# An FFT convolution's last tile: its intermediate results stored and reloaded in seven groups instead of three, and its inverse transform in three parts

## The chip, the cores and the metric

The kernel runs on one core of one Trainium2 chip. The metric is the device time of one execution in microseconds (us). Engines are named as in the profile: PE (TensorE), DVE (VectorE), ACT (ScalarE), POOL (GpSimd) and SP (SyncE, which here only issues DMAs). Every engine works through its own list in order.

## What is computed

A 7 x 7 convolution of a 224 x 224 image with 96 channels, as a product of Fourier transforms. The filter is padded with zeros and the product is circular, so it is a circular convolution:

```python
x: (1, 224, 224, 96) bf16, w: (7, 7, 96, 96) bf16
wp = jnp.pad(w, ((0, H - K), (0, W - K), (0, 0), (0, 0)))
Xf = rfft2(x.astype(float32), axes=(1, 2))
Wf = rfft2(wp.astype(float32), axes=(0, 1))
Yf = jnp.einsum('bhwi,hwio->bhwo', Xf, Wf)
y = irfft2(Yf, s=(H, W), axes=(1, 2)).astype(bfloat16)
```

## The kernel before

The image is cut into 8 bands of 28 rows (NJ, B). Along the rows a short transform of length 34 with 17 frequency slots (NS) is used; along the width the 7 taps are applied directly, with ten taps in a fast form for pairs of pixels. The width is cut into seven tiles of 32 pixels, t = 0 to 6; the last is TL = 6.

Each tile goes through three stages, which overlap between tiles.

- A: PE transforms the rows of x by matmuls with Fm; ACT and DVE evict the result from PSUM into xf. DVE then makes differences and sums of planes (J) by groups of slots (JGB).
- B, `b_round(t, s, ...)`, once for each slot s: PE multiplies the planes with the filter's slots (WF) into two PSUM banks. ACT scales the first bank into a tile `tt__` (in the two real slots, 0 and 16, it copies). DVE makes u and v from `tt__` and the banks. The sum of u and v goes to yf: on DVE in some slots, else on POOL. In the last tile DVE has slots 0, 3, 6, 9, 12 and 14 to 16, and POOL has 1, 2, 4, 5, 7, 8, 10, 11, 13. The rounds of one tile are the slots 0 to 16.
- C: the sums of a group of slots are stored from yf to scratch in DRAM (scr), since the inverse transform contracts over slots and bands and so needs another layout. They are reloaded with bands, slots and real or imaginary part on the partitions; PE multiplies with G; ACT and DVE evict; SP stores to out. For tiles 0 to 5 this work of tile t - 1 is spread over the rounds of tile t as jobs (`c_jobs`), with stores from the buffers yo and J.

The last tile's C stage has no later tile beside which it could run. Its groups of slots are in YGRPL. A group's store is made by `put` at the group's last slot; in the last tile, all but the last are put into the list `puts` and are issued by ACT one round later, right behind the scale of that round, by `puts.pop(0)()`. The last one is issued by SP. The scratch of the last tile is three tensors: slots 0 to 8 (scra, up to SA), 9 to 14 (scrb, up to SB), and 15 and 16 (a second scrb). SP reloads the first in round 11 (SA + 2), in four DMAs; after the rounds `load_b` reloads the second on ACT in two halves, and the third on SP.

The inverse of the last tile is 16 chunks of 384 columns with two matmuls each. `first` multiplies the reloaded slots 0 to 8 (72 partitions: four bands) with GA and needs only the first reload; `second` multiplies slots 9 to 16 (128 partitions: eight bands) with GB and adds to the same PSUM bank. Eight firsts are issued, then WARM = 36 matmuls of 384 columns with zeros that add nothing, then the seconds, each followed by its eviction by DVE or ACT in turn (`tail_evac`) and, after the fourth, by the first of a later chunk. Every second chunk SP stores 768 columns of 112 rows to out. GA and GB are made from G by 20 small DMAs, one for each round of tiles 3 and 4 (`g_parts`).

All engines' lists are in the program's own order (`_Ordered`). An instruction that waits holds all that stand behind it on its engine; a DMA also waits for the DMA eight before it, since eight semaphores are used in turn. PSUM has eight banks, given out in turn by `bank()`.

Of the kernel before, what the change touches and what calls it, by code (L numbers as in the profile page):

```python
# [8 lines left out]
BF16 = mybir.dt.bfloat16  # L9
# [5 lines left out]
B = 28  # L15
L = B + KT - 1
LC = L - 2
NS = L // 2
REAL = (0, NS - 1)
JG = 4  # L20
NJ = 8
# [3 lines left out]
TW = 16  # L25
# [7 lines left out]
NSLOT = 2 + 3 * (NS - 1)  # L33
PGRP = ((0, 5), (5, 8), (8, 11), (11, 14), (14, 17))
YGRP = ((0, 3), (3, 6), (6, 9), (9, 12), (12, 15), (15, 17))
YGRPL = ((0, 3), (3, 6), (6, 9), (9, 12), (12, 15), (15, 17))
SA = 9
SB = 15
YMAX = 3
YBUF = 4  # L40
JGB = ((0, 3), (3, 6), (6, 9), (9, 12), (12, 15), (15, 17))
# [2 lines left out]
SH2 = (0, 8, 13, 17)  # L44
MERGE = ()
NP2 = 0
WARM = 36
FILL = 3
FEV = 4
WMID = 14  # L50
# [16 lines left out]
def kernel(  # L67
# [50 lines left out]
    def bank():  # L118
        return pools["psb"].tile([128, 512], F32, name="pb")
# [36 lines left out]
    KA = 4 * 2 * SA  # L156
    KB = (NJ * 2 * (SB - SA), NJ * 2 * (NS - SB))
    assert sum(KB) == 128
    XW = 2 * TW * C
    xn_bufs = [cpool.tile([R, XW + 32], BF16, name=f"xn{i}") for i in range(2)]  # L160

# [52 lines left out]
    wu = cpool.tile([128, 128], BF16, name="wu")  # L214
# [341 lines left out]
    def b_round(t, s, mid, end, ydve=False, planes=()):  # L556
# [26 lines left out]
        if s in REAL:  # L583
            for part in range(2):
                conv(b0, part * C, 0, part)
            SE.copy(out=tt_[:, 0:2 * C], in_=b0[:, 0:2 * C])
            mid()
            for mi, m in enumerate((2, 1)):
                for part in range(2):
# [52 lines left out]
            load["v"] += (560 if ydve else 250 if t < 2 else 0) + (560 if merge else 900)  # L642
            end()
        if s == y1 - 1:
            dst, yo0 = scr_tiles[t], 0
            if t == TL:
                i = (s >= SA) + (s >= SB)
                dst, yo0 = scr_tiles[(t, i)], (0, SA, SB)[i]
# [25 lines left out]

    TW2 = 2 * TW * C
    tl_all = xf_bufs[(TL + 1) % 2].rearrange("c p r s w j -> c (p r s w j)")
    tl_a = [tl_all[0:KA, g * TW2:(g + 1) * TW2].rearrange("p (w e) -> p w e", e=2 * C) for g in range(2)]
    tl_b = tl_all[:, 2 * TW2:3 * TW2].rearrange("p (w e) -> p w e", e=2 * C)

    def load_b(i, eng, nh):  # L680
        sb = scr_tiles[(TL, 1 + i)].rearrange("w j s (r e) -> (j s r) w e", r=2)
        for h in range(nh):
            w0, w1 = h * TW // nh, (h + 1) * TW // nh
            eng.dma_start(out=tl_b[i * KB[0]:i * KB[0] + KB[i], w0:w1], in_=sb[:, w0:w1])

    def g_parts():
        for j in range(4):
            dma(GA[j * 2 * SA:(j + 1) * 2 * SA, j * B:(j + 1) * B], G[0:2 * SA, 0:B])
            yield
        for j in range(NJ):  # L690
# [128 lines left out]
    for r in range(NS + LAG):  # L819
        if r == 0:  # L820
            for i in range(2, PGRP[0][1]):
                add(2 * i - 4, 2 * i - 3, [diff(i)])
            add(1, 4, fj[1][1])
            add(3, 7, fj[2][1])
        for p in range(3):
            if r == (1, 3, 5)[p]:
                new_xf(1, SH2[p], SH2[p + 1])
                fj = f_jobs(1, p)
                if p == 2:
                    for jg in range(2):  # L830
                        fj[jg][-1] = then_load(fj[jg][-1], 2, jg)
                add(2 * r + 1, 2 * r + (5, 5, 4)[p], fj[0] + fj[1])
        for p in range(3):
            if r == SH2[p + 1] + 1 - (p == 2):
                new_xf(2, SH2[p], SH2[p + 1])
                fj = f_jobs(2, p)
                if p == 2:
                    for jg in range(2):
                        fj[jg][-1] = then_load(fj[jg][-1], 3, jg)
                add(2 * r, 2 * r + (8, 7, 5)[p], fj[0] + fj[1])  # L840
        if r == PGRP[-2][1] + 1:
            assert not any(q[2] for q in qs[:len(PGRP) - 1])
# [5 lines left out]
            GA = g_pool.tile([KA, 4 * B], BF16, name="GA")  # L848
            GB = g_pool.tile([128, 2, 4 * B], BF16, name="GB")
            GE.memset(GA[:], 0.0)  # L850
            GE.memset(GB[:], 0.0)
# [18 lines left out]
    gp = g_parts()  # L870
    for t in range(2, NT):
        if t == TL:
            scr_tiles[t] = None
            scr_tiles[(t, 0)] = dr_pool.tile([TW, NJ, SA, 4 * C], BF16, name="scra")
            for i in range(2):
                scr_tiles[(t, 1 + i)] = dr_pool.tile([TW, NJ, (SB - SA, NS - SB)[i], 4 * C], BF16, name=f"scrb{i}")
        else:
            scr_tiles[t] = dr_pool.tile([TW, NJ, NS, 4 * C], BF16, name="scr")
        qs = []
# [38 lines left out]

    def first(g, q):
        pc = bank()[0:M4, 0:4 * C]  # L920
        TE.matmul(pc, lhsT=GA[:], rhs=tl_a[g][:, 2 * q:2 * q + 2, :].rearrange("p w e -> p (w e)"), start=True, stop=False)
        return pc

    def second(g, q, pc, yo):
        TE.matmul(pc, lhsT=GB[:, g], rhs=tl_b[:, 2 * q:2 * q + 2, :].rearrange("p w e -> p (w e)"), start=False, stop=True)
        tail_evac(yo[0:M4, q % 4 * 4 * C:(q % 4 + 1) * 4 * C], pc, 4 * C)
    order = [(g, q) for h in range(2) for g in range(2) for q in range(4 * h, 4 * h + 4)]
    live = {k: first(*k) for k in order[:8]}
    for _ in range(WARM):
        TE.matmul(live[order[7]].rearrange("p (a b) -> p a b", a=3), lhsT=wu[:, 0:M4], rhs=wu[:].unsqueeze(1).to_broadcast([128, 3, 128]),  # L930
                  start=False, stop=False)
    LF = 4
    for i, (g, q) in enumerate(order):
        if q % 4 == 0:
# [5 lines left out]
        if q % 2 == 1:  # L940
            w0, c0 = TL * 2 * TW + (q - 1) * 4, (q % 4 - 1) * 4 * C
            dma(out[0, g * M4:(g + 1) * M4, w0:w0 + 8, :].rearrange("h w c -> h (w c)"), yo[0:M4, c0:c0 + 8 * C])
    if not NP2:
        ps0_cm.__exit__(None, None, None)

# [29 lines left out]
```

## Time and profile before

| | us |
|---|---|
| median of 3 runs (268.49 to 272.28) | 268.77 |
| the profiled execution, its own time | 269.31 |
| its span, first to last instruction | 267.5 |
| PE busy | 255.1 (95%) |
| DVE busy | 216.2 (81%) |
| ACT busy | 197.6 (74%) |
| POOL busy | 97.7 (37%) |
| round 0 of the last tile: ACT's copy starts | 222.61 |
| round 16 of the last tile: ACT's copy starts | 250.11 |
| first and last store of the last tile's output are issued | 259.56, 263.42 |

The mean granted clock of TensorE is 0.995. DMA moves 46.78 MB at a mean of 175 GB/s. The profile shows one execution. All work has the line of one helper (L101), so that rows are told apart by the names of the tiles: out<-in, partitions x elements, type. A busy time is the time from an instruction's start to its end; instructions of one engine overlap a little, so that starts follow each other faster than the durations tell. "SPq" and "ACTq" are DMA issues.

### The profile page before, as it was taken

To read this page: it belongs to the slowest core of one execution; us is meant where nothing else is said; L and a number is where in the kernel's file an instruction comes from. 1 tells how busy PE (TensorE), PEld (TensorE's weight loads), DVE (VectorE), ACT (ScalarE), POOL (GpSimd) and SP (SyncE) were. 2 spreads that over 40 slices of the span, in tenths; PEclk is the share of its full clock that TensorE was granted. 3 is DMA by queue.
4 is the path that set the end of the run, shared out by engine and by line. 5 is a ranking of instruction groups with operands and counts; after the bars stand their busy time and mean duration, and the time that the engine had idled before them with its cause. 6 is when DMAs were issued, how large, how long until landed. Compare 5 with 4: busy or idle time off the path is not lost. (4 is left out here: it accounts for less than half of the span.)

```text
span 267.5 us, 12139 instructions
## 1 busy us (share of the span) xinstructions
PE 255.1 (95%) x5128; PEld 235.7 (88%) x5128; DVE 216.2 (81%) x465; ACT 197.6 (74%) x485; POOL 97.7 (37%) x152
## 2 busy tenths in 40 slices
PE   8897999999999999999999999999999999999983
PEld 2787999999998999999999998989999889879861
DVE  7997699889899788778887888778888789978523
ACT  8796978497964578998988789886988864187123
POOL 7771324364558344222222322233123323422100
PEclk9999999999999999999999999999999999999998
DMA  8994102711111697987876486979678443887845
GB/s 197 230 251 76 48 2 67 245 45 48 47 48 49 192 258 159 294 238 223 272 195 188 117 235 221 253 216 341 235 152 242 169 128 125 204 250 182 259 107 191
DMA packets 46690, 46.78 MB, mean 175 GB/s; under 512 B 35292, under 2 KB 38056, under 8 KB 46540
## 3 DMA queue, kind: packets, MB, share of 16 engines
q1 hardware_dynamic: 44348, 43.95, 59.6%
q10 hardware_dynamic: 2288, 2.06, 2.6%
q8 instruction: 40, 0.66, 1.1%
q14 instruction: 14, 0.11, 0.2%
HBM read 24.66 MB, written 21.33 MB: 172 GB/s over the span
## 5 line engine op out<-in xcount | busy, mean ns | idle before, releaser
L101 PE MATMUL pb<-WF,J 96*128 96x96 bf16 x2821 | 162.9, 206 | 1.7 <-DVE J L101 1.3
L101 PEld LDWEIGHTS <-J 96*128 96x128 bf16 x2821 | 138.0, 98 | 12.3 <-issue 3.5
L101 POOL TENSOR_TENSOR yf<-v,u 128x384 bf16<-128x384 f32 x79 | 81.3, 1040 | 145.7 <-issue 84.6
L101 ACT CAST xf<-pb 96x408 bf16<-96x408 f32 (+3 forms) x145 | 67.3, 486 | 7.6 <-PE pb L101 3.8
L101 PE MATMUL pb<-WF,xf 96*128 96x96 bf16 x952 | 60.0, 206 | 0.9 <-ACT WF L101 0.9
L101 DVE TENSOR_TENSOR J<-xf 96x1824 bf16<-96x1824 bf16 (+1 forms) x84 | 56.9, 716 | 0.0
L101 PEld LDWEIGHTS <-xf 96*128 96x128 bf16 x952 | 47.2, 98 | 1.3 <-issue 1.2
L101 PE MATMUL pb<-Fm,xn 118*128 118x136 bf16 (+3 forms) x640 | 45.5, 199 | 0.2 <-DVE u L101 0.2
L101 PE MATMUL pb<-tt,Gm 102*84 102x384 bf16 (+1 forms) x132 | 32.9, 326 | 0.6 <-ACT J L101 0.3
L101 PEld LDWEIGHTS <-xn 118*128 118x128 bf16 x640 | 30.3, 97 | 0.3 <-issue 0.3
L101 ACT CAST WF<-pb 96x480 bf16<-96x480 f32 (+1 forms) x58 | 28.6, 558 | 2.3 <-PE pb L101 2.3
L101 ACT CAST J<-pb 84x384 bf16<-84x384 f32 (+1 forms) x65 | 28.1, 490 | 2.6 <-PE pb L101 2.6
L101 ACT CAST yo<-pb 84x384 bf16<-84x384 f32 (+1 forms) x63 | 27.1, 486 | 2.3 <-POOL yf L101 1.3
L101 DVE TENSOR_TENSOR J<-J 96x912 bf16<-96x912 bf16 (+2 forms) x42 | 24.2, 576 | 0.0
L101 PE MATMUL pb<-wq 128*128 128x120 bf16 (+1 forms) x288 | 21.8, 226 | 0.7 <-DMA wq<-in_w_dram 0.6
L101 PEld LDWEIGHTS <-wq 128*128 128x128 bf16 (+1 forms) x288 | 19.9, 148 | 1.7 <-DVE xf L101 1.1
L101 DVE TENSOR_TENSOR yf<-v,u 128x384 bf16<-128x384 f32 x26 | 15.1, 580 | 0.9
L101 PE MATMUL pb<-wu 128*112 128x384 bf16 (+1 forms) x59 | 14.5, 391 | 1.1 <-DVE ct L101 1.1
L101 PEld LDWEIGHTS <-wu 128*112 128x112 bf16 (+1 forms) x59 | 7.4, 127 | 5.6 <-issue 3.1
L101 PEld LDWEIGHTS <-Gm 102*84 102x84 bf16 (+1 forms) x132 | 11.1, 117 | 1.0 <-issue 0.4
L101 ACT COPY xf<-xf 96x816 bf16<-96x816 bf16 (+3 forms) x20 | 11.1, 613 | 0.0
L101 ACT CAST tt<-pb 112x384 bf16<-112x384 f32 x8 | 3.6, 480 | 9.3 <-PE pb L101 9.2
(387 smaller groups left out, 239.2 us busy)
## 6 DMA issues: line engine op xcount, KB each, us to landing
scr<-yf SPq DMA_DIRECT2D x30, 288.0 KB
xn<-in_x_dram SPq DMA_DIRECT2D x12, 672.0 KB
tt<-scr SPq DMA_DIRECT2D x24, 336.0 KB
out_dram<-yo SPq DMA_DIRECT2D x12, 252.0 KB
out_dram<-J SPq DMA_DIRECT2D x12, 252.0 KB
tt<-scr SPq DMA_DIRECT2D x6, 288.0 KB
WF<-in_x_dram SPq DMA_DIRECT2D x2, 672.0 KB
out_dram<-tt SPq DMA_DIRECT2D x8, 168.0 KB
```

Of the source, the lines that this page charges most:

```text
L101: r = fn(*a, **k)
```

## The change

The last tile's slots are stored in seven groups with a scratch tensor each: slots 0 to 2, 3 to 5, 6 and 7, 8 to 10, 11 to 13, 14 and 15, and 16 alone. The groups are reloaded onto the partitions of three parts: part 0 takes the first three groups (128 partitions), part 1 the next two (96), part 2 the last two (48). All eight bands are on the partitions in each. SP reloads the first five groups in the rounds 5, 8, 10, 13 and 16, each at the head of its round; after the rounds ACT reloads slots 14 and 15, and SP slot 16. Round 16 now takes a store from `puts` too, behind its copy. The inverse is 12 chunks of 512 columns with three matmuls each: eight of part 0, eight of part 1, then 7 matmuls of 512 columns with zeros, then those of part 2 with the other parts of the last four chunks between. Output stores alternate between 1024 and 512 columns. G's parts are made by 56 small DMAs in the rounds of tiles 2 to 5. One clear of 128 x 672 on POOL takes the place of two.

```diff
-YGRPL = ((0, 3), (3, 6), (6, 9), (9, 12), (12, 15), (15, 17))
-SA = 9
-SB = 15
+YGRPL = ((0, 3), (3, 6), (6, 8), (8, 11), (11, 14), (14, 16), (16, 17))
+LANE = ((0, 0), (0, 48), (0, 96), (1, 0), (1, 48), (2, 0), (2, 32))
+KP = (128, 96, 48)
+CW = 512
-WARM = 36
+WARM = 7
...
             SE.copy(out=tt_[:, 0:2 * C], in_=b0[:, 0:2 * C])
+            if puts:
+                puts.pop(0)()
             mid()
...
-    def load_b(i, eng, nh):
-        sb = scr_tiles[(TL, 1 + i)].rearrange("w j s (r e) -> (j s r) w e", r=2)
-        for h in range(nh):
-            w0, w1 = h * TW // nh, (h + 1) * TW // nh
-            eng.dma_start(out=tl_b[i * KB[0]:i * KB[0] + KB[i], w0:w1], in_=sb[:, w0:w1])
+    tl_p = [tl_all[:, i * TW2:(i + 1) * TW2] for i in range(3)]
+
+    def load_l(i, eng):
+        (p, l), n = LANE[i], 2 * NJ * (YGRPL[i][1] - YGRPL[i][0])
+        eng.dma_start(out=tl_p[p][l:l + n].rearrange("p (w e) -> p w e", e=2 * C),
+                      in_=scr_tiles[(TL, i)].rearrange("w j s (r e) -> (j s r) w e", r=2))
...
     def g_parts():
-        for j in range(4):
-            dma(GA[j * 2 * SA:(j + 1) * 2 * SA, j * B:(j + 1) * B], G[0:2 * SA, 0:B])
-            yield
-        for j in range(NJ):
-            for i, (s, s1) in enumerate(((SA, SB), (SB, NS))):
-                n = 2 * (s1 - s)
-                dma(GB[i * KB[0] + j * n:i * KB[0] + (j + 1) * n, j // 4, j % 4 * B:(j % 4 + 1) * B], G[2 * s:2 * s1, 0:B])
+        for (p, l), (a, b) in zip(LANE, YGRPL):
+            for j in range(NJ):
+                n = 2 * (b - a)
+                dma(GP[l + j * n:l + (j + 1) * n, p, j // 4, j % 4 * B:(j % 4 + 1) * B], G[2 * a:2 * b, 0:B])
                 yield
...
-            if t in (3, 4):
+            if t < TL:
                 next(gp, None)
-            if t == TL and s == SA + 2:
-                sv = scr_tiles[(TL, 0)].rearrange("w j s (r e) -> (j s r) w e", r=2)
-                for g in range(2):
-                    for p0, p1 in ((0, 64), (64, KA)):
-                        dma(tl_a[g][p0:p1], sv[g * KA + p0:g * KA + p1])
+            if t == TL:
+                for i in range(len(YGRPL) - 2):
+                    if s == YGRPL[i][1] + 2:
+                        load_l(i, DE)
             b_round(t, s, fills(qs, 2 * s), fills(qs, 2 * s + 1), bool(now) or (t == TL and s >= NS - 3), now)
...
-    load_b(0, SE, 2)
-    load_b(1, DE, 1)
+    load_l(5, SE)
+    load_l(6, DE)
...
+    order = [(g, 3 * h + c) for h in range(NC // 3) for g in range(2) for c in range(3)]
+    live = {}
+    for k in order[:8]:
+        live[k] = bank()[0:M4, 0:CW]
+        acc(0, k, live[k])
+    for k in order[:8]:
+        acc(1, k, live[k])
     for _ in range(WARM):
...
     for i, (g, q) in enumerate(order):
...
-        second(g, q, live[(g, q)], yo)
+        acc(2, (g, q), live[(g, q)])
+        tail_evac(yo[0:M4, q % 3 * CW:(q % 3 + 1) * CW], live[(g, q)], CW)
         k = i + 8 - LF
         if 8 <= k < len(order):
-            live[order[k]] = first(*order[k])
+            k = order[k]
+            live[k] = bank()[0:M4, 0:CW]
+            acc(0, k, live[k])
+            acc(1, k, live[k])
```

Here `acc(p, k, pc)` is the matmul of part p of chunk k into the bank pc, and SE, DE, GE are the lists of ACT, SP and POOL.

More of the change, by code (lines that the diff above doesn't have):

```diff
@@ L155 @@
     G = cpool.tile([3 * FR, 3 * B], BF16, name="Gm")
-    KA = 4 * 2 * SA
-    KB = (NJ * 2 * (SB - SA), NJ * 2 * (NS - SB))
-    assert sum(KB) == 128
+    assert all(KP[p] >= l + 2 * NJ * (b - a) for (p, l), (a, b) in zip(LANE, YGRPL))
     XW = 2 * TW * C
@@ L644, in b_round @@
         if s == y1 - 1:
[L645 to L648, printed above, removed]
+            dst, yo0 = (scr_tiles[(t, YGRPL.index((y0, y1)))], y0) if t == TL else (scr_tiles[t], 0)
             def put(eng=DE):
@@ L676 @@
     tl_all = xf_bufs[(TL + 1) % 2].rearrange("c p r s w j -> c (p r s w j)")
-    tl_a = [tl_all[0:KA, g * TW2:(g + 1) * TW2].rearrange("p (w e) -> p w e", e=2 * C) for g in range(2)]
-    tl_b = tl_all[:, 2 * TW2:3 * TW2].rearrange("p (w e) -> p w e", e=2 * C)
-    def load_b(i, eng, nh):
-        sb = scr_tiles[(TL, 1 + i)].rearrange("w j s (r e) -> (j s r) w e", r=2)
-        for h in range(nh):
-            w0, w1 = h * TW // nh, (h + 1) * TW // nh
-            eng.dma_start(out=tl_b[i * KB[0]:i * KB[0] + KB[i], w0:w1], in_=sb[:, w0:w1])
-    def g_parts():
-        for j in range(4):
-            dma(GA[j * 2 * SA:(j + 1) * 2 * SA, j * B:(j + 1) * B], G[0:2 * SA, 0:B])
-            yield
-        for j in range(NJ):
-            for i, (s, s1) in enumerate(((SA, SB), (SB, NS))):
-                n = 2 * (s1 - s)
-                dma(GB[i * KB[0] + j * n:i * KB[0] + (j + 1) * n, j // 4, j % 4 * B:(j % 4 + 1) * B], G[2 * s:2 * s1, 0:B])
+    tl_p = [tl_all[:, i * TW2:(i + 1) * TW2] for i in range(3)]
[3 more added lines that the diff above has]
+                      in_=scr_tiles[(TL, i)].rearrange("w j s (r e) -> (j s r) w e", r=2))
+    def g_parts():
+        for (p, l), (a, b) in zip(LANE, YGRPL):
+            for j in range(NJ):
+                n = 2 * (b - a)
+                dma(GP[l + j * n:l + (j + 1) * n, p, j // 4, j % 4 * B:(j % 4 + 1) * B], G[2 * a:2 * b, 0:B])
                 yield
@@ L847 @@
             g_pool = ctx.enter_context(tc.tile_pool(name="gp", bufs=1, side="right"))
[L848 to L851, printed above, removed]
+            GP = g_pool.tile([128, 3, 2, 4 * B], BF16, name="GP")
+            GE.memset(GP[:], 0.0)
         if r == NS + 3:
@@ L872 @@
         if t == TL:
[L873 to L876, printed above, removed]
+            for i, (y0, y1) in enumerate(YGRPL):
+                scr_tiles[(t, i)] = dr_pool.tile([TW, NJ, y1 - y0, 4 * C], BF16, name=f"scrl{i}")
         else:
@@ L917 @@
     M4 = 4 * B
[L919 to L927, printed above, removed]
@@ L928, with acc @@
-    live = {k: first(*k) for k in order[:8]}
+    NC = TW2 // CW
+    def acc(p, k, pc):
+        g, q = k
+        TE.matmul(pc, lhsT=GP[0:KP[p], p, g], rhs=tl_p[p][0:KP[p], q * CW:(q + 1) * CW], start=p == 0, stop=p == 2)
+    order = [(g, 3 * h + c) for h in range(NC // 3) for g in range(2) for c in range(3)]
[5 more added lines that the diff above has]
+        acc(1, k, live[k])
     for _ in range(WARM):
-        TE.matmul(live[order[7]].rearrange("p (a b) -> p a b", a=3), lhsT=wu[:, 0:M4], rhs=wu[:].unsqueeze(1).to_broadcast([128, 3, 128]),
-                  start=False, stop=False)
+        TE.matmul(live[order[7]].rearrange("p (a b) -> p a b", a=4), lhsT=wu[:, 0:M4], rhs=wur, start=False, stop=False)
@@ L932 @@
     LF = 4
     for i, (g, q) in enumerate(order):
-        if q % 4 == 0:
+        if q % 3 == 0:
             yo = t_pool.tile([128, TW // 2, 2 * C], BF16, name="tt").rearrange("p w e -> p (w e)")
-        second(g, q, live[(g, q)], yo)
+        acc(2, (g, q), live[(g, q)])
+        tail_evac(yo[0:M4, q % 3 * CW:(q % 3 + 1) * CW], live[(g, q)], CW)
         k = i + 8 - LF
         if 8 <= k < len(order):
-            live[order[k]] = first(*order[k])
-        if q % 2 == 1:
-            w0, c0 = TL * 2 * TW + (q - 1) * 4, (q % 4 - 1) * 4 * C
-            dma(out[0, g * M4:(g + 1) * M4, w0:w0 + 8, :].rearrange("h w c -> h (w c)"), yo[0:M4, c0:c0 + 8 * C])
+            k = order[k]
+            live[k] = bank()[0:M4, 0:CW]
+            acc(0, k, live[k])
+            acc(1, k, live[k])
@@ L943 @@
+        if q % 3:
+            c0, c1 = (q - 1 if q % 3 == 1 else q) * CW, (q + 1) * CW
+            dma(out[0, g * M4:(g + 1) * M4, TL * 2 * TW:(TL + 1) * 2 * TW, :].rearrange("h w c -> h (w c)")[:, c0:c1],
+                yo[0:M4, c0 - q // 3 * 3 * CW:c1 - q // 3 * 3 * CW])
     if not NP2:
```

## The prediction

> **What bounds it now.** I read the chain that ended last first, then the timelines of ACT, DVE, POOL and SP over the last 30 us, then the granted clock. The chain (start us, us, what):
>
> ```profile
> 239.10 0.49 DVE v L101
> ...
> 250.84 0.56 DVE yf L101
> ...
> 251.41 4.03 DMA scrb<-yf
> ...
> 255.45 3.04 DMA xf<-scrb
> ...
> 258.53 3.78 PE pb L101 x21
> ```
>
> The last sum of the last tile (slot 16) ends at 251.40. Its store to scratch takes 4.03 us, its reload 3.04 us, then 16 inverse matmuls, evictions and stores run to 267.5. So there are two questions: when do the last sums come, and what lies between them and the last inverse matmuls. ACT and DVE, rounds 8 to 12 of the last tile (ACT row "tt__" = scale of a round; x2 = two casts):
>
> ```profile
> 237.17 0.48 ACT L101 ACTIVATE tt__7103<-pb 128x288 f32<-128x288 f32 x1
> 237.47 0.93 ACT L101 CAST yo<-pb 84x384 bf16<-84x384 f32 x2
> 238.20 0.51 ACT L101 ACTIVATE tt__7153<-pb 128x288 f32<-128x288 f32 x1
> 239.61 0.33 ACTq L101 DMA_DIRECT2D scra<-yf  x1
> 239.97 0.85 ACT L101 CAST yo<-pb 84x384 bf16<-84x384 f32 x2 [1.27 <-POOL yf L101]
> ...
> 244.27 0.47 ACT L101 ACTIVATE tt__7324<-pb 128x288 f32<-128x288 f32 x1
> 244.93 0.33 ACTq L101 DMA_DIRECT2D scrb<-yf  x1
> ```
>
> ```profile
> 244.84 0.36 DVE L101 SCALAR_TENSOR_TENSOR u<-pb,tt__7324 128x192 f32<-128x192 f32 x1 [1.05 <-ACT tt__7324 L101]
> ```
>
> A store that ACT issues blocks ACT until the sums of its group are done: 1.27 us idle before the casts at 239.97. ACT is then packed without a gap until 244.7, and DVE waits 1.05 us for ACT's scale of round 12. From 244.84 to 251.40 DVE has no idle time, so any delay of that scale reaches the last sum whole. POOL's sums matter too:
>
> ```profile
> 237.19 1.00 POOL L101 TENSOR_TENSOR yf<-v,u 128x384 bf16<-128x384 f32 x1 [3.77 <-issue]
> 238.58 1.00 POOL L101 TENSOR_TENSOR yf<-v,u 128x384 bf16<-128x384 f32 x1 [0.39 <-DVE v L101]
> 242.95 1.96 POOL L101 TENSOR_TENSOR yf<-v,u 128x384 bf16<-128x384 f32 x2 [3.37 <-issue]
> 248.18 1.00 POOL L101 TENSOR_TENSOR yf<-v,u 128x384 bf16<-128x384 f32 x1 [3.28 <-issue]
> ```
>
> These are slots 7, 8, 10 with 11, and 13. Third, the clock (column after the engines' shares):
>
> ```profile
> 262.78:264.88 2.10, 0.01 (x1) 0.00 (x0) 0.58 (x2) 0.58 (x2) 0.00 (x0) 1.00 0.85 272
> 264.88:267.40 2.52, 0.00 (x0) 0.00 (x0) 0.00 (x0) 0.00 (x0) 0.00 (x0) 0.50 0.18 60
> ```
>
> PE's last matmul ends at 262.78; 2.10 us later the granted clock is half.
>
> **The stores move against ACT's order.** The groups now end at slots 2, 5, 7, 10, 13, 15, 16 instead of 2, 5, 8, 11, 14, 16, and a store stands behind the scale of the next round. The first two are unchanged.
>
> Round 8: the store of slots 6, 7 waits behind the scale (ends 237.65) for POOL's slot 7, 238.19; with 0.33 of issue ACT goes on at 238.5, 1.05 later than its casts at 237.47. The scale of round 9 goes from 238.20 to about 239.3, and u of round 9 on DVE (0.31 idle before) from 238.81 to 239.9. DVE is nearly without a gap from there, so u of round 10 goes from 242.01 to 243.1, its v ends at 243.9, POOL's slot 10 at 245.0 (before 243.95). The old stall at 239.61 is gone, so ACT's casts after scale 9 are not later than before.
>
> Round 11: the store of slots 8 to 10 stands behind that round's scale (ended 242.94) and waits for slot 10 until 245.0. ACT stands still where it ran four casts (242.80 to 244.43). After 0.33 of issue those take 1.7 (0.88 + 0.90, overlapping): scale 12 starts at 246.9 instead of 244.27, u of round 12 at 247.4 instead of 244.84, +2.55. The old store behind scale 12 falls away; it cost ACT 0.2 of waiting and 0.33.
>
> Round 14: the store of slots 11 to 13 waits for POOL's slot 13, which ends at 249.18 + 2.55 = 251.75. It holds scale 15 until 252.1 (ends 252.5), so u of round 15 starts at 252.6 rather than at 249.52 + 2.55 = 252.07: 0.5 more. The last sum ends at 251.40 + 2.55 + 0.5 = 254.45, +3.05. Bounds: 0, if ACT's casts find slack that I don't see, and +3.5, if PE's full PSUM banks add to it. I take the sum, since each row in it is packed.
>
> **SP's queue.** The reload of slots 11 to 13 is issued in round 16 ahead of the last slot's store, and waits for its own store to land. Nearest row: the 288 KB store issued at 249.68 let the reloads go at 252.00, 2.32 us; the other bound is the 4.03 of the chain. With 2.32 the reload is issued at 251.75 + 2.32 = 254.1, takes 0.6 of SP (xf<-scra rows: four in 2.56), and the last store goes at 254.7, only 0.25 behind its sum. The reloads of earlier groups also hold SP, with C stores behind them: priced under the fourth rival.
>
> **Transfers.** The last hop moves 96 KB instead of 192. Store: rows 2.32 (288 KB alone) and 4.03 (192 KB behind others); it now lies behind a 288 KB reload in the same queue: 2.8 taken, bounds 2.0 to 4.03. Reload: 3.04 for 192 KB, half the runs: 2.6 taken, bounds 2.2 to 3.04. Last reload lands at 254.7 + 2.8 + 2.6 = 260.1. The hop itself is 5.4 instead of 7.1, 1.7 saved.
>
> **But PE does not wait for that alone.** The second part's eight matmuls and seven warming ones stand ahead of the last part's, behind the reload of slots 11 to 13. That one has 288 KB: bounds 3.04 (192 KB) and 5.96 (the last xf<-scra, behind three others); I take 3.9, since another store shares the engines. It lands at 258.0. A matmul of 384 columns streams in 0.162 (36 in 6.01), so 512 take 0.216, and 15 take 3.24: the last part starts at 261.25 at full clock, later than 260.1.
>
> And the clock will not be full. The first part's eight matmuls need PSUM banks that the last rounds free by about 254.5; then PE is idle until 258.0, 3.3 us, longer than the 2.10 after which it fell above. At the start of the kernel 14 matmuls of 512 columns took 5.36 us instead of 3.2, so some ten ran at half rate, 2.2 us lost. Here the loss lies between 0 and 2.2, or 3.24 if all 15 run at half; I take 1.6, as part of the half-rate time passes while PE is idle. Last part's start: 262.85 against 258.53, +4.3.
>
> The Trainium skill, "TensorE: Matmul & The Clock Gate", Part 1, puts the throttle behind at least one idle window of about 3.4 us; by it a gap of 3.3 us would leave the clock up, and the 1.6 would fall away. The trace disagrees: half clock 2.10 us after the last matmul.
>
> **The output phase.** Twelve evictions of 512 columns for sixteen of 384: DVE 0.55 to about 0.69, ACT 0.48 to 0.60 (its 96x512 cast row), six each, 4.1 for 4.4; but four chunks now carry three matmuls (0.65 a chunk, before 0.33). The 8 output stores keep their bytes, the last has 112 KB for 168. Both phases are about 4.9 from first matmul to last store: -0.1 taken, -0.4 to +0.5.
>
> **Small edits.** G's parts come in 56 small loads, not 20; SP issues one in 0.62 to 0.88. The tile that held 17 of them took 126.58 to 158.38, 31.8 us; the one with none 190.90 to 222.61, 31.7. PE's work covers them: +0.2 for 36; without that cover, 36 x 0.75 = 27 us of SP. The one larger POOL clear (184 and 278 ns before) lies in idle POOL time: 0.
>
> Sum: 4.3 - 0.1 + 0.2 = +4.4. The profiled execution took 269.31 (span 267.5), so 273.7; against the median of 268.77, 273.2.
>
> **Rivals.**
> 1. The forecast, chance 0.50: 273.2, own range 271.3 to 275.4.
> 2. The clock stays up, because the eight first matmuls spread into the gap or the gap is shorter: +2.8, 271.6. For it: 64% of PE's time in 22.50 to 25.90 was enough to hold it. Against: the 2.10 us row. 0.16. The page's rule above gives this time too.
> 3. Not slower: ACT's waits are absorbed and the last sum stays at 251.40. Then slots 11 to 13 are stored at 249.2, reloaded from 251.5, landed at 255.4 (3.9) or 254.6 (3.04); 3.24 of matmuls end at 258.6 or 257.8, and the last reload lands at 252.1 + 2.8 + 2.6 = 257.5. Against 258.53 that is +0.1 to -0.7: 268.1 to 268.9. It decides if scale 12 starts before about 245. For it: ACT is only 74% busy. Against: the packed rows. 0.13. Much below that nothing can go, since the saved 1.7 is all that the hop gives.
> 4. The reloads clog SP: five now stand among the C stores of rounds 5 to 16. In the trace an output store went only at 247.32, behind the four reloads, though its casts ended at 243.68: 3.6 us. If such a wait withholds an output buffer from ACT in rounds 9 to 12, up to 2.6 more: 275.8. 0.21.
>
> **Numbers.** 273.2, range 269.3 to 276.4: it reaches toward the third and past the fourth. 2%, about what a measurement of this kernel can tell from no change, is 5.4 us: slower if over 274.1. The fourth (0.17 of 0.21) and the upper end of the first (0.20 of 0.50) give slower 0.37; faster 0.03; within 0.60.
>
> **What would show it.** The chain ends through the reload of slots 11 to 13 and PE, not through the last slot's reload; ACT idle some 2 us before a store in round 11; DVE waiting over 2 us for scale 12; the last sum near 254.4; clock 0.50 in part of the last 15 us before the last part's matmuls. If ACT has no such wait, the forecast is wrong at its root; if the last sum is late and the clock stays at 1.00, the second case holds.

## The result and the profile after

| | before | after |
|---|---|---|
| median of 6 runs each (lowest to highest), us | 269.29 (268.49 to 272.28) | 288.26 (283.56 to 290.84) |
| the profiled execution, its own time | 269.31 | 290.75 |
| its span | 267.5 | 289.0 |

The changed kernel is slower: 1.0595 times the time of before, 95% interval 1.0473 to 1.0718. The forecast was 273.2, the range ended at 276.4. The ratios here leave out executions more than 1.5% above the fastest of their kernel, medians do not, and the profiled execution of after is one of those, so its 21.5 us over before hold some 5 us more than the 16 for which the ratio stands.

The first reading is where the 21.5 us between the two spans lie. Marks that exist in both traces cut the span: the first scale or copy of a tile on ACT, the scale of slot 8 in the last tile, the end of the last sum, the first matmul of the last inverse part, the last instruction.

| us | before | after | difference |
|---|---|---|---|
| start to tile 2 | 95.9 | 97.1 | 1.2 |
| tiles 2 and 3 | 62.5 | 62.5 | 0.0 |
| tile 4 | 32.5 | 37.4 | 4.9 |
| tile 5 | 31.7 | 38.7 | 7.0 |
| last tile, to the scale of slot 8 | 14.6 | 14.6 | 0.0 |
| scale of slot 8 to the end of the last sum | 14.2 | 17.0 | 2.8 |
| last sum to the first matmul of the last part | 7.15 | 11.6 | 4.45 |
| last part's first matmul to the end | 8.94 | 10.09 | 1.15 |

More than half lies in tiles 4 and 5, where the prediction had 0.2. The first row is no effect of the change: over the 14 profiled executions of this study it lies between 95.0 and 98.0. In six of them, after among them and before not, the granted clock stood at 0.50 for 3.4 us near 26 us; these six have 97.1 to 98.0, the others 95.0 to 96.8.

The chain of waits of after (start us, us, what) holds, in tile 5, things that the chain of before does not hold at all, and ends with the last tile:

```profile
197.69 6.14 DMA out_dram<-yo
...
205.03 2.51 DMA scr<-yf
...
207.56 3.75 DMA tt<-scr
...
211.35 7.29 PE pb L102 x83
...
264.52 4.45 DMA scrl<-yf
...
269.03 3.59 DMA xf<-scrl
...
272.66 11.48 PE pb L102 x33
```

An output store holds ACT's buffer; then tile 4's last store to scratch leaves SP at 205.03, its reload at 207.56, and PE can only go on at 211.35. PE's timeline shows the hole. The matmul that waits there belongs to the inverse of tile 4, and it holds the matmuls of tile 5 behind it:

```profile
206.89 0.46 PE L102 MATMUL pb<-WF,J 96*128 96x96 bf16 x7
211.35 0.86 PE L102 MATMUL pb<-tt,Gm 102*84 102x384 bf16 x2 [4.00 <-DMA tt<-scr]
```

Before, the same reload left SP 3.9 us after the start of tile 5, not 10.5, and landed 3.1 us before PE needed it (201.27, the same matmul):

```profile
191.05 0.35 SPq L101 DMA_DIRECT2D scr<-yf  x1
194.81 5.02 SPq L101 DMA_DIRECT2D tt<-scr  x6
```

```profile
201.27 0.49 PE L101 MATMUL pb<-tt,Gm 102*84 102x384 bf16 x2
```

SP's timeline in tile 4 of after shows what was in front of the stores and reloads:

```profile
167.53 0.69 SPq L102 DMA_DIRECT2D GP<-Gm  x1
169.24 0.35 SPq L102 DMA_DIRECT2D out_dram<-yo  x1
169.63 0.68 SPq L102 DMA_DIRECT2D GP<-Gm  x1
170.43 0.38 SPq L102 DMA_DIRECT2D scr<-yf  x1
171.01 1.41 SPq L102 DMA_DIRECT2D GP<-Gm  x2
172.53 0.40 SPq L102 DMA_DIRECT2D out_dram<-J  x1
```

A G load takes 0.68 of SP where a store of 288 KB takes 0.35. The end of the chain is what the prediction had drawn: the store of slots 11 to 13, its reload, PE. ACT's timeline of after, for the rounds 8 to 12 that the prediction shows of before, and for round 15 behind them:

```profile
250.31 0.49 ACT L102 ACTIVATE tt__7144<-pb 128x288 f32<-128x288 f32 x1
251.06 0.33 ACTq L102 DMA_DIRECT2D scrl<-yf  x1
251.43 0.85 ACT L102 CAST yo<-pb 84x384 bf16<-84x384 f32 x2 [0.63 <-PE pb L102]
...
256.67 0.85 ACT L102 CAST J<-pb 84x384 bf16<-84x384 f32 x2 [2.29 <-PE pb L102]
257.42 0.42 ACT L102 ACTIVATE tt__7305<-pb 128x288 f32<-128x288 f32 x1
257.80 0.33 ACTq L102 DMA_DIRECT2D scrl<-yf  x1
...
259.66 0.44 ACT L102 ACTIVATE tt__7362<-pb 128x288 f32<-128x288 f32 x1
...
264.52 0.33 ACTq L102 DMA_DIRECT2D scrl<-yf  x1
264.97 0.41 ACT L102 ACTIVATE tt__7501<-pb 128x288 f32<-128x288 f32 x1 [2.77 <-DVE yf L102]
```

The scale of slot 12 (tt__7362) comes 9.35 after that of slot 8 (tt__7144), where it came 7.10 after it before. But the wait that makes it late is not at the store of round 11 (257.80, straight behind its scale): ACT stood 2.29 us ahead of a cast into J. The row names PE; the chain runs through "250.42 6.17 DMA out_dram<-J", the store that has to empty that buffer. It left 14.7 us after the start of the last tile, where it left at 12.9 before. SP had been done with the reload ahead of it at 249.23 and then waited, by the semaphore records, until 250.36 for the landing of the DMA eight places back, a store of ACT. PE and the granted clock (columns of the windows: PE's busy time and count, PEld, DVE, ACT, POOL, then the clock, DMA's share, GB/s):

```profile
267.40 0.38 PE L102 MATMUL pb<-xf,GP 128*112 128x512 bf16 x1 [0.46 <-DVE yf L102]
272.66 3.66 PE L102 MATMUL pb<-xf,GP 96*112 96x512 bf16 x8 [4.88 <-DMA xf<-scrl]
276.12 2.90 PE L102 MATMUL pb<-wu 128*112 128x512 bf16 x7
278.95 5.62 PE L102 MATMUL pb<-xf,GP 48*112 48x512 bf16 x20
```

```profile
268.30:271.77 3.47, 0.00 (x0) 0.00 (x0) 0.00 (x0) 0.00 (x0) 0.00 (x0) 1.00 0.49 130
271.77:278.59 6.82, 5.93 (x14) 3.10 (x15) 0.00 (x0) 0.00 (x0) 0.00 (x0) 0.50 0.20 48
278.59:285.42 6.83, 5.98 (x22) 2.06 (x20) 3.86 (x6) 3.31 (x6) 0.00 (x0) 1.00 0.44 134
```

All 15 matmuls ahead of the last part run at half clock, and the full clock comes back as they end.

### The profile page after: what moved, and what is told of

It reads as the page before. It is cut to its first block, busy times and chain, and to the rows that moved or that the text cites. A ratio compares the mean times of both kernels' runs of the same rounds, so it can differ in the third digit from the quotient of the medians.

```text
span 289.0 us, 12122 instructions
## 1 busy us (share of the span) xinstructions
PE 265.4 (92%) x5103; PEld 238.5 (83%) x5103; DVE 216.6 (75%) x463; ACT 197.0 (68%) x483; POOL 98.6 (34%) x151
## 5 line engine op out<-in xcount | busy, mean ns | idle before, releaser
L102 PE MATMUL pb<-WF,J 96*128 96x96 bf16 x2821 | 166.1, 208 | 2.9 <-DVE J L102 2.0
L102 PEld LDWEIGHTS <-J 96*128 96x128 bf16 x2821 | 140.8, 99 | 15.9 <-issue 6.4
L102 PE MATMUL pb<-WF,xf 96*128 96x96 bf16 x952 | 60.9, 208 | 0.9 <-ACT WF L102 0.9
L102 PE MATMUL pb<-Fm,xn 118*128 118x136 bf16 (+3 forms) x640 | 46.6, 201 | 1.4 <-ACT yo L102 1.2
L102 PE MATMUL pb<-tt,Gm 102*84 102x384 bf16 (+1 forms) x132 | 34.3, 334 | 5.0 <-DMA tt<-scr 4.0
L102 ACT CAST yo<-pb 84x384 bf16<-84x384 f32 (+1 forms) x63 | 27.1, 488 | 11.1 <-DMA out_dram<-yo 5.8
L102 PEld LDWEIGHTS <-xn 118*128 118x128 bf16 x640 | 31.4, 99 | 1.7 <-issue 1.7
L102 DVE TENSOR_TENSOR J<-J 96x912 bf16<-96x912 bf16 (+2 forms) x42 | 24.2, 577 | 0.0
L102 PE MATMUL pb<-xf,GP 128*112 128x512 bf16 (+2 forms) x36 | 11.7, 447 | 5.4 <-DMA xf<-scrl 4.9
L102 ACT CAST tt<-pb 112x512 bf16<-112x512 f32 x6 | 3.3, 587 | 16.3 <-PE pb L102 16.3
L102 DVE CAST tt<-pb 112x512 bf16<-112x512 f32 x6 | 3.9, 686 | 14.0 <-PE pb L102 14.0
L102 PEld LDWEIGHTS <-GP 128*112 128x112 bf16 (+2 forms) x36 | 4.6, 146 | 11.7 <-DMA xf<-scrl 6.0
```

Of the source, the lines that this page charges most:

```text
L102: r = fn(*a, **k)
```

## The experiments

For tiles 4 and 5, theory U: the 36 added G loads take SP's time in tiles where SP has none to spare. Rival: the seven groups and their waits do it. For the tail: ACT's wait at its stores, the clock, the weight loads.

### The loads taken out, and put into the kernel before

In the first, all 56 loads are made in nine transfers:

```diff
-            for j in range(NJ):
-                n = 2 * (b - a)
-                dma(GP[l + j * n:l + (j + 1) * n, p, j // 4, j % 4 * B:(j % 4 + 1) * B], G[2 * a:2 * b, 0:B])
-                yield
...
+            n = 2 * (b - a)
...
+            src = G[2 * a:2 * b, 0:B]
+            dma(bass.AP(g0.tensor, g0.offset + l * GW + p * NJ * B, [[GW, n], [n * GW + B, NJ], [1, B]]),
+                src.unsqueeze(1).to_broadcast([n, NJ, B]))
+            yield
+        dma(GP.rearrange("q p h m -> q (p h m)"), gimg[:])
...
```

> The changed kernel, with the 56 small loads of the G matrices (one 28-column block each, from the G matrix to GP) replaced by nine: GP's zeros are written to an image of GP in DRAM, seven transfers (one for each group of slots) write that group's eight blocks into the image, and one loads the image into GP. The computation is the same. Theory U (SP's issue time is what tiles 4 and 5 lost): 47 issues of some 0.68 us fewer, 32 us of SP; tiles 4 and 5, 37.4 and 38.7 us long with the change and 32.5 and 31.7 before, come back to 32 to 33 each, and the time falls by 11 to 13 us to about 275 (273.5 to 276.5). Rival (the seven groups themselves, or their waits, make tiles 4 and 5 long): the time stays at 284 to 290 and tile 4 and 5 at 36 or more. In both, the end of the kernel is as with the change: from the end of the last sum to the first matmul of the last part 11 to 12 us, all 15 matmuls before it at half clock.

Measured: 276.57 (ratio to before 1.0215, 1.014 to 1.0289). Tile 4 took 32.2, tile 5 31.7: all of the loss there is gone, and the seven groups have no part in it. The tail is as in after: 17.1, 11.2 and 10.1 us.

The second adds the loads to the kernel before:

```diff
+    def g_more():
+        yield from g_parts()
+        for _ in range(2):
+            yield from g_parts()
...
-            if t in (3, 4):
+            if t < TL and nmore[0] < 56:
+                nmore[0] += 1
                 next(gp, None)
```

> The kernel before, with each round of tiles 2 to 5 issuing one G load until there have been 56: its own 20, and 36 repeats of them that write the same values again. Nothing else is changed: three scratch parts, no waiting ACT stores, no third inverse part. Theory U: SP's queue loses some 24 us as in the changed kernel, tiles 4 and 5 come out at 36 to 39 us each, and the time is 278 to 283. Rival (the loss needs the seven groups): 268 to 271 with tiles 4 and 5 at 31 to 33.

Measured: 279.48 (1.0346, 1.0288 to 1.0404); tiles 4 and 5 took 37.0 and 36.9. The loads alone make 9.7 of the 11.9 us that the two tiles lost in after.

### Is it the issue, or the place among eight?

Each DMA waits for the one eight before it to land. So a load costs SP the time of its issue, and it also holds one of eight places until it has landed. This run keeps the number and more than halves the issue (its edit against the run with 36 repeats):

```diff
-        for _ in range(2):
-            yield from g_parts()
+        for k in range(36):
+            dma(gpad[:, k * B:(k + 1) * B], x[0, 0:6, k, 0:B])
+            yield
```

> The kernel before, with 36 more small loads after its own 20, one per round as in the run with 36 repeats, but of 6 rows from the input in DRAM into a tile that nothing reads: the same number of DMAs, each with an issue of some 0.3 us (the 6-row loads of the input take 0.27 to 0.33) where a G load from the G matrix takes 0.68. It tells two forms of theory U apart. U1 (what is lost is SP's time at each issue): 11 us of SP instead of 24; tiles 4 and 5 come out at 32 to 34 us each, the time at 269.5 to 273. U2 (what is lost is the number of DMAs: each waits for the landing of the one eight before it, by the eight semaphores that the program hands round): the same loss as with the 36 repeats, tiles 4 and 5 at 36 to 37 us each, the time at 278 to 281.

Measured: 278.10 (1.0335, 1.0273 to 1.0398); the added loads were issued in 0.32 at the median. Tile 4 took 33.8, tile 5 38.2: together 7.8 over before where the 36 repeats had 9.7, with half the issue time. U1 is wrong as the only cause. SP's timeline in tile 4 of this run:

```profile
164.37 0.35 SPq L101 DMA_DIRECT2D scr<-yf  x1
164.76 0.33 SPq L101 DMA_DIRECT2D gpad<-in_x_dram  x1
166.90 0.33 SPq L101 DMA_DIRECT2D out_dram<-yo  x1
167.28 0.30 SPq L101 DMA_DIRECT2D gpad<-in_x_dram  x1
167.87 0.35 SPq L101 DMA_DIRECT2D scr<-yf  x1
168.99 0.60 SPq L101 DMA_DIRECT2D gpad<-in_x_dram  x2
```

The issues are short now, and gaps of up to 1.8 us stand between them. In the semaphore records, ten of SP's waits in tile 4, 7.9 us, end within 0.1 us of the landing of the DMA eight back. Next, the same 36 are issued by ACT, so that they are not on SP's queue at all (its edit against this run):

```diff
-            dma(gpad[:, k * B:(k + 1) * B], x[0, 0:6, k, 0:B])
+            SE.dma_start(out=gpad[:, k * B:(k + 1) * B], in_=x[0, 0:6, k, 0:B])
```

> As the kernel before with 36 cheap loads (278.1), but ACT issues the 36, in the same rounds, and SP only its own. The program still gives them places in the same rotation of eight semaphores. U2 (the rotation of eight): the loss stays, since SP's next transfer still waits for the one eight back, and ACT now waits in it too: 276 or more, tiles 4 and 5 together 70 us or more. U1' (SP's queue alone: its issues and what stands behind them): tiles 4 and 5 at 32 to 33 us each and 269 to 272, with 11 us of ACT's idle time used.

Measured: 286.66 (1.0628, 1.0542 to 1.0714); tiles 3, 4 and 5 took 39.3, 36.5 and 37.8. What SP waited for in tiles 3 and 4 (us in total, times, longest):

```profile
SPq L101 <- DMA gpad<-in_x_dram: 20.5, 10, 4.3
SPq L101 <- DMA tt<-scr: 10.0, 8, 1.9
```

SP issued none of these loads and waited 20.5 us for them, since SP cannot pass the place that a load holds. That ACT issues them late, behind its other work, would explain why the waits are so long; it was not tried. The places alone, with no issue on SP, make such a loss (ACT's own 36 issues, some 11 us, may add to it in this run). It does not follow that issue time is free: in after, SP issued for 29.3 of tile 4's 37.4 us and waited only 3.4 for places. The two fill the same time, and cutting one lets the other take it. Their shares in after are not separated.

### How many, and where?

> The kernel before with 18 repeats of G loads instead of 36, one in every second round after its own 20. Proportion (each extra load costs its 0.29 us, 10.6 us for 36): 274 to 275. A limit (an extra DMA costs nothing until the eight that may be on their way are used up, and its full place in the row from then on): tile 4, which had 40 DMAs in 32.5 us before and 53 in 37.0 with 36 repeats, stays at 32.2 to 33, tile 5 likewise, and the time is 268.5 to 271.

The edit against the run with 36 repeats:

```diff
-        for _ in range(2):
-            yield from g_parts()
+        for i, _ in enumerate(g_parts()):
+            yield
+            if i >= 17:
+                break
+            yield
```

Measured: 277.41 (1.0254, 1.0188 to 1.032); tiles 4 and 5 took 33.4 and 38.4. Both expectations missed: half the loads make 7.6 of the 9.7 us from tile 2 to tile 6. But all these runs also begin in tile 2, where the kernel before has no loads. That alone:

```diff
-            if t in (3, 4):
+            if t < TL:
```

> The kernel before with its own 20 G loads, no more, begun in the first round of tile 2 instead of tile 3, as the changed kernel and all the runs with extra loads have it. In those the last store of tile 2 to scratch left 10 to 11 us after its round, where it left 2.2 in the kernel before. P (it is the place, loads in tile 2, and not the number): tiles 4 and 5 come out long as with 18 extra, and the time is 274 or more. N (the number: a list that is late after tile 2 catches up when the loads end): the store of tile 2 late by 7 to 11 us, those of tiles 3 and 4 by under 4, tiles 4 and 5 at 31.7 to 32.6, and the time 268 to 270.5.

Measured: 269.38 (0.9987, 0.9948 to 1.0026): no difference. The store of tile 2 was late by 10.5, those of tiles 3 and 4 by 4.0 and 2.9. So it is not the start in tile 2, and the loss is more like a step than in proportion: none without added loads, 7.6 us with 18, 9.7 with 36. Whether their number counts, or that they reach into tiles 4 and 5 (SP issued 13 loads there with 18 more, 7 in the kernel before, none in this run), these runs do not separate. This table sums up the six kernels (times from the profiled executions; "late" is from ACT's copy of slot 16 to the issue of that tile's last store; "places" is SP's wait that the landing of the DMA eight back ended):

| | DMAs of SP in tile 4 | issue, us | places, us | late: tile 2, 3, 4 | tiles 4 + 5 |
|---|---|---|---|---|---|
| before | 40 | 24.2 | 2.2 | 2.2, 7.3, 2.7 | 64.2 |
| its 20 loads from tile 2 on | 32 | 21.2 | 0.0 | 10.5, 4.0, 2.9 | 64.3 |
| 18 more | 42 | 23.5 | 3.9 | 11.2, 9.7, 9.3 | 71.8 |
| 36 more, cheap | 49 | 21.5 | 7.9 | 11.4, 10.3, 10.5 | 72.0 |
| 36 more | 53 | 29.4 | 3.7 | 11.1, 13.8, 10.9 | 73.9 |
| after | 54 | 29.3 | 3.4 | 10.2, 13.3, 11.1 | 76.2 |

SP's list may be 7 to 10 us late at the end of a tile and catch up. If it is still 9 us late at the end of tile 4, the reload of that tile comes after tile 5's PE needs it, and 4.6 to 5.9 us are lost in that one place (between the scales of slots 6 and 7 of tile 5, in all four of the long ones). In the kernel before PE comes to it 10.4 us after the start of tile 5; it landed at 7.2 and 7.4 in the two short kernels of the table and at 13.6 to 14.3 in the four long ones. That is where a step can come from.

The pause is not the whole loss in tile 5. In each of the four the granted clock fell to 0.50 within 1 us of the pause's end, for 3.4 us in the run with 36 repeats and for 6.8 in the others; in the kernels that lost nothing there it did not fall in tiles 4 and 5. An estimate: PE's pause plus half of the time for which PE was busy at half clock.

| us, tile 5 | pause | PE busy at half clock | pause + half of it | loss |
|---|---|---|---|---|
| 18 more | 3.7 | 6.7 | 7.1 | 6.7 |
| 36 more, cheap | 3.4 | 6.1 | 6.4 | 6.5 |
| 36 more | 3.3 | 3.4 | 5.0 | 5.2 |
| after | 4.0 | 5.8 | 6.9 | 7.0 |

By it a third to a half of tile 5's loss is the clock's, and that 18 loads cost tile 5 more than 36 repeats is mostly the clock too.

One more run did the reverse, with the 20 loads of before in seven transfers:

> The kernel before, with its 20 small G loads replaced by seven transfers through an image in DRAM. U: SP in the kernel before stood just short of its limit (tile 4 took 32.5 us with 7 G loads in it, and 32.2 in the kernel with nine loads), so the gain is 0.3 to 0.6 us, not measurable against runs that spread over 3. Rival (the 20 loads already cost what they hold up, in proportion to the 36: 5 us): 264 to 266.

Measured: 268.70 (1.0000, 0.9964 to 1.0036): tile 4 is 0.3 shorter, and no gain can be measured.

### The tail, step by step

From the kernel with nine G loads on, each run adds one edit to the run before. First, three of the stores go from ACT to SP:

```diff
-            if t == TL and s < NS - 1:
+            if t == TL and s < NS - 1 and s not in (7, 10, 13):
                 puts.append(lambda: put(SE))
```

> As the kernel with nine G loads, and the stores of the last tile's groups that end at slots 7, 10 and 13 are issued by SP at the end of their round, where ACT issued them one round later. Theory A (ACT waits in its queue for POOL's sums at these stores, and scales come late by it): from the scale of slot 8 to the end of the last sum 14 to 15 us where the changed kernel takes 17.1, and the time is 2 to 3 us below the kernel with nine G loads, at about 272. Rival (SP, now waiting for the same sums, issues reloads and output stores late instead): within 0.7 us of the kernel with nine G loads, or slower.

Measured: 276.76 (1.0246, 1.0193 to 1.0298), the same as without it. From the scale of slot 8 to the last sum it is 15.85 for 17.1; the next run, with the same stores, has 16.3, so ACT's waits at stores are worth 0.7 to 1.2 in single profiles. Its wait for J stayed, as its timeline shows:

```profile
241.21 0.41 ACT L102 ACTIVATE tt__7212<-pb 128x288 f32<-128x288 f32 x1
244.39 0.85 ACT L102 CAST J<-pb 84x384 bf16<-84x384 f32 x2 [2.77 <-DMA out_dram<-J]
```

Here the row names the transfer itself. Next, the clock:

```diff
+    for _ in range(20):
+        TE.matmul(live[order[7]].rearrange("p (a b) -> p a b", a=4), lhsT=wu[:, 0:M4], rhs=wur, start=False, stop=False)
```

> As the kernel with nine G loads and the three stores on SP, and 20 more matmuls of zeros (512 columns each) between the eight of the first inverse part and the eight of the second, while PE waits for the reload of slots 11 to 13. Theory C (the 15 matmuls ahead of the last part run at half clock because PE stood still during that wait): the clock is 1.00 when the last part's matmuls begin or shortly before, the eight of part 1 and the seven zeros take 3.2 us and not 6.6, and the time is 2.5 to 3.5 us below the kernel with the three stores on SP, at about 269. Rival 1 (the clock falls all the same, because the idle time lies ahead of the zeros): within 0.7 us. Rival 2 (the end waits for the load of the last slot, not for PE): within 0.7 us, with the clock up.

Measured: 272.94 (1.0115, 1.007 to 1.0161), 3.8 less at the median. The clock was 1.00 from 245 to 267 us, past the last matmul, and from the last sum to the last part it took 7.9 us for 11.1. PE's timeline:

```profile
252.54 4.48 PE L102 MATMUL pb<-wu 128*112 128x512 bf16 x20
256.85 1.89 PE L102 MATMUL pb<-xf,GP 96*112 96x512 bf16 x8
258.58 1.68 PE L102 MATMUL pb<-wu 128*112 128x512 bf16 x7
260.19 5.62 PE L102 MATMUL pb<-xf,GP 48*112 48x512 bf16 x20
```

The 15 matmuls that took 6.3 us in after take 3.3. The last line still has 5.62 at full clock, and the next edit is aimed at it:

```diff
-KP = (128, 96, 48)
+KP = (128, 96, 96)
```

> As the kernel with nine G loads, stores on SP and 20 zeros, with the last inverse part's 20 matmuls reading 96 rows instead of 48 (the weights of the added rows are zero, so the result is the same). In the last part the weight load before a 48-row matmul that follows a 96-row one, and the load of 128 rows that follows a 48-row one, start only when the matmul before has gone in; three matmuls take 0.92 us where three of 512 columns at full clock take 0.64. Theory K (the switch from 96 or 128 rows to 48 and back keeps the weight load from being done ahead): three take 0.64 to 0.70, the last part is 0.8 to 1.2 us shorter (from its first matmul to the end 10.1 us before this edit, 8.9 to 9.3 after), the time falls by about 1 to some 272. Rival (the evictions of 512 columns, 0.59 on ACT and 0.69 on DVE, or PE's wait for a bank set the pace): no change of the last part beyond 0.2.

PE's timeline, the line that answers to the last one above:

```profile
262.06 4.57 PE L102 MATMUL pb<-xf,GP 96*112 96x512 bf16 x20
```

The last part took 9.2 for 10.15, as theory K has it. The time did not show it (273.41; 1.0178, 1.0135 to 1.022): this profiled execution reached tile 2 at 97.6, the one of the run before at 95.0, and such a scatter is larger than the gain. Then the reloads:

```diff
-                    if s == YGRPL[i][1] + 2:
+                    if s == (9, 12, 13, 13, 16)[i]:
```

> As the kernel with 96 rows, and the reloads of the last tile's first five groups are queued on SP at rounds 9, 12, 13, 13 and 16 instead of 5, 8, 10, 13 and 16, behind the output stores of the tile before. Theory S (ACT waits ahead of the scales of slots 11 and 12 for J's buffer, whose store to the output stands on SP behind reloads that wait for a store to land): J's store is issued 12.9 to 13.5 us after the start of the last tile instead of 14.2 to 16.0, ACT's wait before the scale of slot 12 is gone, and from the scale of slot 8 to the end of the last sum it is 14.2 to 15.0 us instead of 16.35; the time falls by 1.4 to 2 to about 270. Rival (something else holds ACT there, or the late reloads now keep the last inverse waiting): no gain, or slower by the time by which the first part's matmuls come late.

Measured: 273.00 (1.0134, 1.0066 to 1.0202). J's store left 12.9 us after the start of the last tile (14.2, 14.5 and 13.3 in the three runs before it), ACT's wait for J was 0.74 (2.77, 3.26 and 1.64), and from the scale of slot 8 to the last sum it took 14.0 (15.85, 16.3 and 14.7). The later the store, the longer the wait and the later the last sum, in all four, so theory S is right about the sums; that the run before already had 14.7, with no edit there, shows how far single profiles scatter. But the first part now waits for its own late reload (PE idle 1.87), the last part starts 10.0 after the last sum, and nothing is gained. PE's timeline:

```profile
251.84 1.91 PE L102 MATMUL pb<-xf,GP 128*112 128x512 bf16 x8 [1.87 <-DMA xf<-scrl]
```

The last run, on the kernel with 96 rows, has the last store on ACT and one zero for seven:

```diff
-WARM = 7
+WARM = 1
...
-                put()
+                put(SE if t == TL and s == NS - 1 else DE)
```

> As the kernel with 96 rows (273.4, its last tile 47.0 us from its first scale to the last instruction), with the last slot's store issued by ACT, behind the store of slots 14 and 15, instead of by SP, where it stands behind the reload of slots 11 to 13 and left 3.9 us after the last sum; and one zero matmul instead of seven ahead of the last part. Theory L (with the clock up, the last part starts when the last slot has been stored and reloaded, and when the eight matmuls of the second part and the zeros are through): the store leaves within 0.5 us of the last sum, the last part starts 7.0 to 7.4 us after the last sum instead of 8.6, the time falls by 1.2 to 1.6. Rival (the reload of slots 11 to 13, which the second part's eight wait for, sets the end: 5.3 us after the last sum, and 1.7 for the eight): the same 7.0 to 7.3 by PE alone, with the store's place worth nothing; the two differ in what PE waits for ahead of the last part. Or, with fewer zeros, the clock falls: 9 to 10 us.

PE's timeline between the first part and the second:

```profile
253.24 4.48 PE L102 MATMUL pb<-wu 128*112 128x512 bf16 x20
260.50 3.66 PE L102 MATMUL pb<-xf,GP 96*112 96x512 bf16 x8 [2.78 <-DMA xf<-scrl]
```

Measured: 276.24 (1.0245, 1.0173 to 1.0316), at the median 2.8 more than with 96 rows alone. The last store did leave at once, but three reloads then went out together, and that of slots 11 to 13 landed 7.5 us after the last sum instead of 5.3; PE stood still after its zeros, and the clock fell. Theory L is wrong: PE waits for slots 11 to 13. No run beats the kernel before.

## Why the prediction was wrong

**The step that failed** is "PE's work covers them: +0.2 for 36; without that cover, 36 x 0.75 = 27 us of SP". It measured 11.9 in the profiles, tiles 4 and 5 together; the loads alone, in the kernel before, 9.7 from tile 2 to tile 6. The case without cover was named with its 27 us, but no rival and no chance stood for it. The cover was read from the lengths of two tiles, 31.8 with 17 loads and 31.7 with none. SP's rows have 13 of the 20 loads in the first of these and 7 in the tile between, which took 32.52. The lengths show that SP had slack for those loads, not how much was left. The rows to read were SP's own: 40 DMAs and 24.2 us of issue in tile 4, and the last store of tile 3, 7.3 us late against 2.2 to 2.8 for those of tiles 2, 4 and 5. The lateness that those loads made was there, and 12 to 20 loads a tile for three tiles kept it from being made up. That a DMA waits for the one eight back was set down with the kernel, and was not used for the price. What a late reload does to the clock (table above) was not in the sum either.

**ACT's stores in rounds 8, 11 and 14.** The size was right by luck, the cause for the most part not: +2.8 measured for +3.05. In round 8 the casts came some 0.8 late for 1.05. In round 14 ACT waited at the store as said. The wait in round 11 did not occur, because ACT had stood still one round earlier, for J's buffer. Taking the stores from ACT gave back 0.7 to 1.2; with the reloads queued behind the output stores as well, all of it was gone. That is the mechanism of the fourth rival (reloads ahead of output stores, a buffer withheld from ACT in rounds 9 to 12), held apart from the forecast when it was part of it.

**The reload of slots 11 to 13 and PE** set the end, as forecast, not the last slot's. Two terms were too small. The store took 4.45 where 2.32 was taken (4.03 was the other bound), so the reload landed 5.3 after the last sum and not 3.55. The 15 matmuls took 6.3 where 4.84 was taken (3.24 + 1.6): all ran at half clock, the upper bound that the text names. The run with 20 zeros shows that it is the clock, and the second case, in which it stays up, is wrong. The Trainium skill, "TensorE: Matmul & The Clock Gate", Part 1, asks for an idle window of about 3.4 us; here PE had nothing to do in 268.30 to 271.77, and the clock fell at its end. So here the trace agrees; in the forecast the gap had been put at 3.3 (258.0 less 254.5 is 3.5), and it was 4.9. But the 2.10 us that the prediction read from before is no length after which the clock falls: it is what was left of the stretch from 261.47 to 264.88, in which PE was busy for 1.32. The last section has the other falls.

**The output phase** was taken as -0.1 with +0.5 as bound, and measured +1.15. The term counted three matmuls of 0.216 a chunk (0.65); they take 0.92. The run with 96 rows shows why: 48-row matmuls among 128- and 96-row ones. The Trainium skill, "TensorEngine Tiling (Array Packing)", Key Properties, says that a change of the tiling mode drains the TensorE, and its section Available Configurations lists tiles of 64 rows among the modes; the trace agrees, if a matmul of 48 rows counts as one of those. Before, 72 and 128 rows alternated at no such price.

**The third case** (not slower) failed with ACT's waits. Without the G loads at all the tail would still have cost 8.1 in the profile (17.1 + 11.2 + 10.1 against 14.2 + 7.15 + 8.94), not 4.4: the time of that kernel, 276.57, is also just above the range.

## What to carry to other kernels

An added DMA is priced by the row of its queue in the busiest stage (issue time, waits for a place, how late the stage's last store leaves), never by the length of a stage that hid earlier ones; cover that has hidden 20 may be used up by them. And a pause of the TensorE can cost more than its length, where the clock falls behind it. Where an engine waits for a buffer, look for the store that empties it and for what stands ahead of that store. Splitting a final transfer into more stores and reloads puts them into queues in which others wait; here it paid in no run, not even with the matmuls behind the reloads at full clock.

## What the runs showed of the hardware

- A load of a few rows from the G matrix to GP, GA or GB, all in SBUF, took SP 0.68 (after) and 0.75 (before) to issue at the median; one of 6 rows from DRAM 0.32 (36 cheap loads), and one with eight blocks from G to DRAM 0.32 (nine loads).
- Such loads hold their place long for their size: 336 bytes or less were 3.3 to 3.9 us from issue to landing at the median (by the semaphore records, tiles 3 to 5), where the stores to scratch of 192 and 288 KB took 4.7.
- A matmul of 48 rows next to ones of 96 and 128 costs about 0.27 us for each set of three (0.92 for 0.65): its weight load and the next one start only when the matmul before is nearly through. With 96 rows 20 matmuls took 4.57 for 5.62, at the same clock.
- In after, the clock changes at 5.53, 26.01, 29.42, 176.19, 179.61, 210.33, 217.15, 271.77, 278.59 and 285.42: all a whole number of 3.41 us apart. The Trainium skill, "TensorE: Matmul & The Clock Gate", Part 1, has a free-running window of that length, and the trace agrees; but by it the window before a fall is idle, and in 206.92 to 210.33 PE was still busy for 0.43 us when the clock fell for the next 6.8:

```profile
206.92:210.33 3.41, 0.43 (x11) 0.29 (x7) 1.18 (x3) 0.93 (x4) 1.82 (x2) 1.00 0.53 130
210.33:217.15 6.82, 5.80 (x58) 5.20 (x59) 3.80 (x7) 2.52 (x6) 0.00 (x0) 0.50 0.85 163
```

- Such a window need not be idle by far. With each of the 14 traces cut at its own changes of the clock into steps of 3.41 us, the clock fell after every step in which PE had been busy for less than 2.0 us (0 to 1.91) and after none with more than 2.73; between the two it sometimes fell and sometimes stayed. In after it fell at 176.19 behind 2.14 us of work, and in before at 264.88 behind 1.32. From half clock it came back only behind steps in which PE had been busy for 3.3 us or more.
